# A second level of Strassen's algorithm for four of the seven products of the first GEMM, with the other three in lasting PSUM banks

## The chip, the cores and the metric

The kernel runs on one core of one Trainium2 chip. The metric is the device time of one execution in microseconds (us). The kernel before takes 662.47 us (median of 3 runs, 661.76 to 662.52). "Faster" or "slower" needs 2%. The experiments ran in several rounds, each beside the kernel before, whose median was 662.5 to 664.65 us in them. So a difference of 2 or 3 us between runs of different rounds is not clear of noise.

## The reference, cut to what matters

```python
state = gamma * state + k[t] (outer) v[t]        # retention: 4 batches, 8 heads, 768 steps, head size 64
y[t]  = scale * q[t] @ state
x = y.transpose(0, 2, 1, 3).reshape(3072, 512)   # 3072 tokens, model size 512
h = x @ w_in                                     # first GEMM, 512 -> 2048
g = where(h > 0, h, exp(min(h, 0)) - 1)          # ELU
out = g @ w_out                                  # second GEMM, 2048 -> 512
```

Everything is fp32. The kernel computes the retention in chunks on TensorE, and the two GEMMs in six blocks of 512 tokens each.

## The kernel before

The first block is computed plainly. From the second block on both GEMMs use Strassen's algorithm, in its form with 7 products in place of 8. From the third block on, the second GEMM has a second level of it: each of its seven products (called groups below) is again made of seven small products. The first GEMM has one level, for each quarter n (0 to 3) of the hidden columns. One quarter is this sequence; `use` runs the ELU on a finished result:

```python
def strassen(product, use, between):
    yield
    pa = bank("a"); product(1, pa, True); m1 = kept(pa)          # ScalarE copies M1 out of PSUM
    yield
    pb = bank("b"); product(2, pb, True); use("C11", plus(pb, m1))   # VectorE adds, ELU begins
    yield
    product(6, pa, False); u2 = kept(pa)                         # accumulates M6 on M1
    yield
    pd = bank("d"); product(7, pd, True)
    yield
    product(5, pa, False); u4 = kept(pa); use("C22", plus(pd, u4))
    yield "gap"
    product(3, pa, False); use("C12", pa)
    yield
    product(4, pd, False); h = plus(pd, u2)
    yield "last"
    use("C21", h)
```

So a quarter releases its four ELUs one after the other, and ELUs of one quarter run beside the products of the next. An ELU is two ScalarE instructions (relu, exp) and a last step on VectorE, which is held back until the next ELU. After C12 of a quarter, VectorE makes T3 and T1, inputs of the second GEMM. In the second GEMM one group is (cut):

```python
product(j, 1, pa, True);  m1 = copy(pa)          # ScalarE, 128x128
product(j, 2, pb, True);  add(res[:, 0, 0], pb, m1)
product(j, 6, pa, False); u2 = copy(pa)          # same bank: waits for the copy of product 1
product(j, 7, pd, True)
product(j, 5, pa, False); add(res[:, 1, 1], pd, copy(pa))
product(j, 3, pa, False); nc.scalar.copy(res[:, 0, 1], pa)
product(j, 4, pd, False); add(res[:, 1, 0], pd, u2)
```

## Time and profile before

| | before |
|---|---|
| time, median | 662.47 us |
| TensorE busy | 637.3 us, 97% of the span |
| VectorE / ScalarE / GpSimd busy | 434.7 / 228.3 / 23.8 us |
| TensorE instructions (matmul) | 6144 |
| a block of tokens | 101.7 to 102.9 us |

In the views PE is TensorE (PEld its weight loads), DVE VectorE, ACT ScalarE, POOL GpSimd and L265 a line of that run's kernel. A line of a timeline has the start and length in us, the engine, the line, the operation, the tiles (written <- read), the shapes, and in brackets the idle time before it and what ended it ("issue" where the profile shows nothing). The seam is the place where the first GEMM of a block ends and its second begins.

What the kernel does not do is wait. The view of TensorE's waits of the kernel before says for whom it waited: us in total, how often, the longest. (The whole view has nine rows.)

```profile
PE sc L265 <- DMA qk<-in_qkv_dram: 8.9, 2, 7.5
PE pa L385 <- DVE xb L342: 2.8, 2, 1.4
...
PE pa L618 <- ACT ms L626: 0.4, 1, 0.4
```

The first two rows are the start of the kernel. At the place that this change touches, the second GEMM's wait for ScalarE's small copies (tile `ms`), there is one wait of 0.4 us in the whole run.

### The profile page before, as it was taken

The page shows a single profiled execution, that of the slowest core. Times are in us where ns is not written, and L with a number is a line of the kernel's source. Part 1 is how long each engine was busy: PE and PEld are TensorE (multiplying, and loading weights), DVE is VectorE, ACT ScalarE, POOL GpSimd, SP SyncE. Part 2 cuts the span into 40 slices and gives each one's busy share as a digit, 9 for nine tenths or more (in the row PEclk, how much of TensorE's full clock was granted, in tenths as well). Part 3 has the DMA queues.
Part 4 walks back from the last instruction along what each step waited for, and adds up shares of the span by engine and source line. Part 5 has one row for each costly group of instructions (what it writes and reads, how often), then busy time and mean ns, then how long its engine had stood idle before and what let it go on. Part 6 is the DMA issues. An engine that isn't in the chain of part 4 may idle for free.

```text
span 658.9 us, 14662 instructions
## 1 busy us (share of the span) xinstructions
PE 637.3 (97%) x6144; PEld 537.5 (82%) x6144; DVE 434.7 (66%) x769; ACT 228.3 (35%) x432; POOL 23.8 (4%) x28
## 2 busy tenths in 40 slices
PE   4799999999999999999999999999999999999997
PEld 4664445458888888889999889999889999888996
DVE  5798688566757644549856457867447958355974
ACT  7477542014431002543112554111455111445211
POOL 1000100001100000200000200000100000000000
PEclk9999999999999999999999999999999999999999
DMA  8658977549114757605767703777801768200693
GB/s 342 235 166 289 343 228 232 143 133 376 72 65 160 255 211 257 254 1 174 223 206 254 251 1 95 228 228 253 301 2 42 242 206 267 96 1 20 222 305 126
DMA packets 63825, 123.64 MB, mean 188 GB/s; under 512 B 5136, under 2 KB 22544, under 8 KB 61712
## 3 DMA queue, kind: packets, MB, share of 16 engines
q1 hardware_dynamic: 63760, 122.70, 55.6%
q8 instruction: 49, 0.80, 0.5%
q14 instruction: 16, 0.13, 0.1%
HBM read 100.66 MB, written 22.02 MB: 186 GB/s over the span
## 4 chain that ended last, share of the span: by engine, by line
PE 95%; DVE 2%; DMA 1%; issue 1%; SPq 0%; ACT 0%; DVEq 0%
PE pa L497 21%; PE pa L618 15%; PE pd L497 10%; PE pd L618 8%; PE hp L396 6%; PE pb L497 5%; PE pa L410 4%; PE pa L555 4%; PE pb L618 4%; PE pd L555 2%; PE kv L287 2%; PE pb L410 2%; PE pd L410 2%; PE y L335 2%; PE sc L265 2%; PE y L311 2%
## 5 line engine op out<-in xcount | busy, mean ns | idle before, releaser
L452 DVE TENSOR_TENSOR h<-pd,m 128x512 f32<-128x512 f32 x42 | 29.1, 692 | 86.1 <-ACT m L447 68.6
L447 ACT COPY m<-pa 128x512 f32<-128x512 f32 x63 | 36.3, 577 | 109.7 <-PE pa L497 73.7
L626 ACT COPY ms<-pa 128x128 f32<-128x128 f32 x84 | 22.3, 265 | 125.3 <-PE pa L618 122.3
L374 ACT ACTIVATE r<-r 128x512 f32<-128x512 f32 x96 | 60.5, 630 | 3.0
L618 PE MATMUL pd<-ts,wq 128*128 128x128 f32 x448 | 59.9, 277 | 0.3 <-DVE res L630 0.3
L618 PE MATMUL pa<-ts,wq 128*128 128x128 f32 x448 | 59.2, 275 | 0.0
L373 ACT ACTIVATE r<-h 128x512 f32<-128x512 f32 x60 | 37.9, 631 | 57.2 <-DVE h L452 57.2
L618 PEld LDWEIGHTS pd<-ts,wq 128*128 128x128 f32 x448 | 54.5, 192 | 1.2 <-DVE res L630 0.9
L618 PEld LDWEIGHTS pa<-ts,wq 128*128 128x128 f32 x448 | 54.8, 192 | 0.2
L618 PE MATMUL pa<-gC,wq 128*128 128x128 f32 x384 | 52.0, 278 | 0.4 <-ACT ms L626 0.4
L376 DVE SCALAR_TENSOR_TENSOR gC<-r,h 128x512 f32<-128x512 f32 x60 | 42.1, 701 | 11.3 <-ACT r L374 11.3
L618 PEld LDWEIGHTS pa<-gC,wq 128*128 128x128 f32 x384 | 47.2, 192 | 1.7 <-ACT ms L626 0.5
L239 POOL TENSOR_TENSOR kvn<-kvn,vf 128x512 f32<-128x512 f32 x20 | 21.8, 1089 | 455.7 <-DMA kvn<-in_qkv_dram 455.7
L497 PE MATMUL pa<-xb,w_s 128*128 128x256 f32 x160 | 37.8, 379 | 0.0
L497 PE MATMUL pa<-xb,w_a 128*128 128x256 f32 x160 | 37.8, 379 | 0.0
L497 PE MATMUL pa<-xt,w_s 128*128 128x256 f32 x160 | 37.8, 379 | 0.0
L497 PE MATMUL pb<-xb,w_a 128*128 128x256 f32 x160 | 37.8, 379 | 0.0
L497 PE MATMUL pd<-xt,w_s 128*128 128x256 f32 x160 | 37.8, 379 | 0.0
L497 PE MATMUL pa<-xt,w_b 128*128 128x256 f32 x160 | 37.8, 379 | 0.0
L497 PE MATMUL pd<-xt,w_b 128*128 128x256 f32 x160 | 37.8, 379 | 0.0
L630 DVE TENSOR_TENSOR res<-pd,ms 128x128 f32<-128x128 f32 x56 | 16.1, 287 | 28.8 <-PE pd L618 26.3
L497 PEld LDWEIGHTS pb<-xb,w_a 128*128 128x128 f32 x160 | 30.4, 190 | 4.1
(121 smaller groups left out, 1092.7 us busy)
## 6 DMA issues: line engine op xcount, KB each, us to landing
wq<-scratch_dram SPq DMA_DIRECT2D x196, 256.0 KB, 4.0
wraw<-in_w_dram SPq DMA_DIRECT2D x16, 1024.0 KB, 6.0
qk<-in_qkv_dram SPq DMA_DIRECT2D x24, 512.0 KB, 8.7
kvn<-in_qkv_dram SPq DMA_DIRECT2D x24, 512.0 KB, 9.4
scratch_dram<-so SPq DMA_DIRECT2D x22, 512.0 KB, 3.4
ws<-scratch_dram SPq DMA_DIRECT2D x7, 1024.0 KB, 7.0
scratch_dram<-w_s SPq DMA_DIRECT2D x8, 512.0 KB, 7.3
out_dram<-res SPq DMA_DIRECT2D x12, 256.0 KB, 3.4
```

Of the source, the lines that this page charges most:

```text
L239: eng.tensor_tensor(out=kv[:, 1], in0=kv[:, 1], in1=vf[:, i].unsqueeze(2).to_broadcast([C, H, D]), op=ALU.mult)
L373: nc.scalar.activation(r, h, AF.Relu, scale=-1.0)
L374: nc.scalar.activation(r, r, AF.Exp, scale=-1.0)
L376: later.append(lambda: nc.vector.scalar_tensor_tensor(g, r, -1.0, h, ALU.add, ALU.max))
L396: nc.tensor.matmul(hp, lhsT=w[n][:, fi, j // 2, j % 2, :], rhs=xb[:, j, :], start=(j == 0), stop=(j == 3))
L410: nc.tensor.matmul(ops[d], lhsT=wo[:, row, d * P : (d + 1) * P], rhs=g_plain[row * NF + f], start=(f == 0 and row == 0), stop=(f == NF - 1 ...
L447: nc.scalar.copy(m, ps)
L452: nc.vector.tensor_tensor(out=h, in0=ps, in1=m, op=ALU.add)
L497: nc.tensor.matmul(ps[:, fi, :], lhsT=w[:, fi, j2, :], rhs=x[:, j2, :], start=(begin and fi == 0 and j2 == 0), stop=(j2 == 1), skip_group_ ...
L555: nc.tensor.matmul(ps[:, d, :], lhsT=ws[:, 2 * d + f // 4, f % 4, :], rhs=gq[INPUT2[j]][:, f, :], start=(begin and f == 0 and d == 0), sto ...
L618: nc.tensor.matmul(ps, lhsT=w[:, f, :], rhs=ts[j][k][:, f, :], start=(begin and f == 0), stop=(f == 3), skip_group_check=True,)
L626: nc.scalar.copy(m, ps)
```

## The change

The intent: in the four blocks that have the second level in the second GEMM, give it to M2, M3, M4 and M7 of the first GEMM as well, to save TensorE time. A second-level product covers all four quarters at once, so results no longer come quarter by quarter. M1, M6 and M5 stay in one level and accumulate in four PSUM banks (`qa`), one for each quarter, that last for the whole first GEMM. VectorE adds each bank to the stored partial result when its turn comes (`first_end`), and then the ELU starts. The last VectorE steps of two ELUs are now held back, where it was one (the 2 in `elu(g, g, 2, ...)`). The core of the diff:

```diff
+    TWICE = [2, 3, 7, 4]
+    PLAN = {2: (None, "C11"), 3: (None, "C12"), 7: (None, "C22"), 4: ("C22", "C21")}
+    def first_twice(tb, j):                       # seven small products, as in the second GEMM
+        ...
+    def first_end(n, name, ps):
+        g = gq[name][:, 2 * n : 2 * n + 2, :]
+        nc.vector.tensor_tensor(out=g, in0=ps, in1=g, op=ALU.add)
+        ...
+        return lambda: elu(g, g, 2, combine if name == "C12" else None)
 ...
-        for n in range(NQ):
-            cur = first(n)
 ...
+        for n in range(NQ):
+            qa.append(ps_r.tile([P, 2, TH], FP32, name="qa", tag="r"))
+            first_rest(n, 1, qa[n])               # M1
+        for at, j in enumerate(TWICE):            # M2, M3, M7, M4 in two levels
+            cur = first_twice(tb, j)
+            ...                                   # C11 ends here: its addition and ELU
+        first_rest(0, 6, qa[0])                   # M6, then C21 ends
+        first_rest(1, 6, qa[1])
+        first_end(0, "C21", qa[0])()
+        first_end(1, "C21", qa[1])()
+        sec = second_twice(...); next(sec)        # four subtractions for the second GEMM
+        for n in (2, 3):
+            first_rest(n, 6, qa[n]); first_end(n, "C21", qa[n])()
+        for n in range(NQ):
+            first_rest(n, 5, qa[n])               # M5, then C22 and C12 end
+            for name in ("C22", "C12"):
+                held_elu.append(first_end(n, name, qa[n]))
+                if n < 3:
+                    held_elu.pop()()
+        next(sec)                                 # products 1, 2 of the second GEMM
+        for e in held_elu: e()                    # the last two ELUs
+        next(sec)                                 # products 6, 7
```

(Some lines of it are joined here.) In the second block GpSimd makes the second-level weights and a DMA writes them to DRAM.

## The prediction

> **What bounds the kernel now.** I read the page first (engine shares, chain of waits), then the windows of one block, then the timeline of each engine across the seam between the two GEMMs.
>
> ```profile
> PE 637.3 (97%) x6144; PEld 537.5 (82%) x6144; DVE 434.7 (66%) x769; ACT 228.3 (35%) x432; POOL 23.8 (4%) x28
> ...
> PE 95%; DVE 2%; DMA 1%; issue 1%; SPq 0%; ACT 0%; DVEq 0%
> ```
>
> The second line is the chain that ended last: 95% of the span is TensorE work, so matmul time saved is time saved, as long as nothing else takes its place. The windows below are block 3 (the first of four that change): its first GEMM with a little of the second, then the rest of the second with the retention of the next block. Columns: length, busy us of PE, PEld, DVE, ACT, POOL, clock, DMA share, GB/s.
>
> ```profile
> 251.60:301.70 50.10, 50.10 (x241) 44.34 (x240) 27.13 (x41) 24.85 (x43) 4.17 (x4) 1.00 0.44 158
> 301.70:352.00 50.30, 48.97 (x846) 47.65 (x846) 39.67 (x81) 8.19 (x28) 0.00 (x0) 1.00 0.70 221
> ```
>
> VectorE has 23 us of slack in the first window and 10 us in the second. A block takes 101.7 to 102.9 us (from the starts of consecutive blocks at 251.76, 353.42, 456.07 and 558.95 in the chain). What a product costs is in the starts of consecutive groups on TensorE:
>
> ```profile
> 253.32 1.89 PE L497 MATMUL pb<-xb,w_a 128*128 128x256 f32 x8
> 255.05 1.89 PE L497 MATMUL pa<-xt,w_s 128*128 128x256 f32 x8
> ...
> 304.57 1.06 PE L618 MATMUL pa<-gC,wq 128*128 128x128 f32 x8
> 305.46 1.06 PE L618 MATMUL pb<-gC,wq 128*128 128x128 f32 x8
> ```
>
> Start to start, a product of the one-level form (four fp32 matmuls of 256 columns, eight records) is 1.727 us; one of the two-level form (four of 128 columns) 0.893 us, 3.4% dearer per column.
>
> VectorE and ScalarE pacing, at a later seam:
>
> ```profile
> 400.75 0.69 DVE L452 TENSOR_TENSOR h<-pd,m 128x512 f32<-128x512 f32 x1 [3.06 <-ACT m L447]
> 401.36 0.68 DVE L376 SCALAR_TENSOR_TENSOR gC<-r,h 128x512 f32<-128x512 f32 x1
> 401.96 0.68 DVE L607 TENSOR_TENSOR ts<-gC 128x512 f32<-128x512 f32 x1
> 402.68 0.69 DVE L607 TENSOR_TENSOR ts<-gC,ts 128x512 f32<-128x512 f32 x1
> ...
> 401.48 0.63 ACT L373 ACTIVATE r<-h 128x512 f32<-128x512 f32 x1 [0.76 <-DVE h L452]
> 402.14 0.63 ACT L374 ACTIVATE r<-r 128x512 f32<-128x512 f32 x1
> 402.68 0.25 ACT L626 COPY ms<-pa 128x128 f32<-128x128 f32 x1
> ```
>
> A 512-wide VectorE operation costs 0.61 us start to start, 0.72 if it reads the result of the one before it. A relu starts 0.72 us after the add that feeds it, its exp 0.66 later, the next ScalarE instruction 0.54 after that.
>
> [...] no instruction of either engine stands ahead of program order. So a small copy behind ten ELUs waits for all ten. [...] In this trace 32 score matmuls took 1.13 us right after the 7.50 us wait at the start, 64 of them 1.16 us later on[...]; no idle time later in this trace is longer than 1.5 us. [...] GpSimd worked from 268.23 for 1.04 us, and the subtraction for T3 that started at 268.66 took 1.16 us in place of some 0.7.
>
> **The change part by part.**
>
> *TensorE, removed and added.* Per block the first GEMM had 28 one-level products, 28 x 1.727 = 48.35 us. Now M1, M5 and M6 stay (12 x 1.727 = 20.72) and M2, M3, M4, M7 become 4 x 7 = 28 two-level products of 0.893 (25.00). Together 45.72: 2.63 us less a block, 10.5 us in four blocks. This is all there is to win, bar some small gaps: 1.6%.
>
> *VectorE, added.* Before, per block: 12 sums from PSUM, 16 last steps of ELU, 8 subtractions for T3 and T1, 4 for the inputs: 40 x 0.61 = 24.4 us. After: 12 sums plus 4 lifts with an addend (M4), 16 additions of the lasting banks, 16 ELU ends, 8 and 4 as before, 8 for the inputs of the second level (4 of them in the second GEMM of the block before): 68 x 0.61 = 41.5 us. So about 17 us more, in a first GEMM that is 2.6 us shorter; with the 39.4 of the second GEMM VectorE goes from 64% to about 83% of a block. On average that still fits. Where it lies decides.
>
> *The seam.* Only C11 can be finished early. All twelve ELUs of C21, C22 and C12 come after the last two-level product. Set 0 at its end (M4's product 3). TensorE still has two M6 and four M5 products, 6 x 1.727 = 10.36 us, then products 1 and 2 of the second GEMM, to 12.15. Its product 6 accumulates in the bank of product 1, so it needs ScalarE's copy of product 1. In program order VectorE does from 0.2 on: 1 lift, 4 additions of C21, 4 subtractions for the second GEMM's input, 5 ELU ends (the last of C11, all of C21); 4 additions of C22 and C12 for n = 0 and 1; the ELU ends of C22 and C12 and T3, T1 for n = 0, the ELU end of C22 for n = 1; the addition of C22 for n = 2. That is 24; the 25th is the addition of C12 for n = 2. It starts at 0.2 + 24 x 0.61 + 0.4 (four dependent neighbours) = 15.2. Its relu 15.9, exp 16.6, then the copy at 17.1 to 17.4. TensorE was ready at 12.15: **5.2 us of idle**, each block. Next, the two ELUs that were held back stand before the copy of product 6: five VectorE operations later, at 18.5, comes the addition of C12 for n = 3; relu 19.8 (behind the ELU of C22), exp 20.5, copy 21.0 to 21.3; products 6 and 7 end at 19.2: **2.1 us**. From there VectorE is about 9 us behind and works without pause (inputs, T3 and T1, the four additions into C11, inputs again, the mask of the scores). What TensorE waits for then: C11 before the third group, about 0.3; M2's sums before products 4 and 7 there, 0.45 and 1.05; the next group 0.6: **2.4 us**. With the 8.3 us of a group against some 6 us of VectorE work it has caught up in the fourth or fifth group.
>
> *The middle.* From the first C11 on, ScalarE has relu and exp before the copy of M7's product 1, which must be done before its product 6: addition 0.8 us after the end of M3's product 5, relu +0.72, exp +0.66, copy +0.54, done +0.63 = 3.35, while products 1, 4 and 2 cover 2.68: **0.7 us**. The one-slot distances elsewhere (0.58 us copies in a 0.89 us slot) just hold.
>
> *Sum of one block*: 5.2 + 2.1 + 2.4 + 0.7 = 10.4 lost, 2.6 won: 7.8 longer. Last block: no retention, and it already loses some 3 us to VectorE (the chain of before there goes through the additions into C11 and the inputs twice), so I take 1.5 off: 6.3.
>
> *Second block* (once): weights of the second level are made by GpSimd, 16 operations of 1.09 us or so (its scaling row), in turns with VectorE (up to 0.5 us each on it, where it has 15 us of slack), then 4 MB are written out and the fetch of the first w_out piece waits behind them. The last can be ready near 180, and with 7.0 us to landing comes at about 188 to 191, when it is wanted at 190.6: 0 to 2 us, I take 1. The reads, 16 x 256 KB more a block, are 4.2 MB: 42 GB/s more on 188, with slots at 342 seen; hidden.
>
> Total: 662.5 + 3 x 7.8 + 6.3 + 1 = 693. I go a little under, to 690, because the four small waits after the seam are the least sure.
>
> **The rivals.** *TensorE stays the bound.* If VectorE's extra work hides, the time is 662.5 - 10.5 = 652. For it: 23 us of slack in the first GEMM's window. Against it: the slack is spread evenly there, the new work is not; it would need the m1 copy to pass ten ELUs. *Only the two waits at the seam hurt and VectorE's lag is absorbed*: 4 x (7.3 + 0.7 - 2.6) = +21.6, so 684. *The long idle also drops the clock*: products 6 and 7 at half rate are 1.8 us more, but most of that lies inside the next wait; up to 2 us a block: 700. *Small weights come late*: eleven slots cover 9.8 us against 4.0 us from issue to landing: no wait expected.
>
> **Range and chances.** The two waits at the seam follow from counting instructions; I trust them to 1.5 us a block, hence 6 in all; the lag after it could be half or double (-5, +8). 80%: 672 to 702. A miss would most likely be to the faster side, if an order I read wrongly spares the seam. Over 2% faster needs 649.2, below even the first rival: 0.03. Slower by over 2% is above 675.7: 0.78. Within: 0.19.
>
> **What would show it.** TensorE's share falls from 97% to about 91%. Per block: one idle gap of some 5 us on TensorE released by ScalarE's copy to the small tile, then one of 2 us, behind ELU instructions; in the windows of the second GEMM VectorE busy throughout its first 20 us. Product spacings still 1.727 and 0.893, so that outside the gaps a block has 2.6 us less of TensorE work. VectorE's total about 500 us. I am wrong if those gaps are absent (then about 652), or if the copy is released by TensorE and not by an ELU; if the gaps are there but the groups after them run without waits, it is the second rival.

## The result, and the profile after

The kernel after takes **701.9 us** (median of 4 runs, 701.14 to 702.46), beside 662.5 us (661.76 to 663.42) of the kernel before in the same rounds. The ratio is 1.059 (95% interval 1.0575 to 1.0612): slower. A ratio here is always the mean time of one kernel's runs over that of the other's of the same rounds, so it is not quite the ratio of the medians that are quoted.

Engine shares and the chain of waits of the kernel after, from its page:

```profile
PE 643.2 (92%) x6528; PEld 550.8 (79%) x6528; DVE 510.2 (73%) x881; ACT 229.4 (33%) x432; POOL 47.4 (7%) x44
...
PE 73%; DVE 20%; issue 3%; ACT 2%; DMA 1%; SPq 0%; DVEq 0%
```

VectorE has 75 us more work, and a fifth of the path to the end now leads over it. TensorE's busy time should have fallen by 10 us and rose by 6 (at the half clock, shown below, a product is busy for 2.08 us in place of 1.06). Its waits, same view as above:

```profile
PE pa L765 <- ACT ms L773: 25.0, 9, 5.8
...
PE pa L684 <- ACT m L697: 2.1, 4, 0.5
PE pa L684 <- DVE m L695: 1.8, 3, 0.8
```

The row that stood at 0.4 us now stands at 25.0, and its longest wait is 5.8 us. The span grew from 658.9 to 700.0 us. From the starts of the blocks, the four changed blocks are 9.5, 10.0, 9.8 and 9.4 us longer than before (38.7 together). Block 2 is 0.9 us longer, and the opening of the kernel, which has not changed, 1.5 us.

One changed block, cut into three windows at the two ends of the seam between the GEMMs (columns: length, then busy us of PE, PEld, DVE, ACT, POOL, the clock, DMA share, GB/s):

```profile
365.31:412.30 46.99, 45.23 (x322) 42.40 (x322) 27.61 (x44) 15.24 (x27) 4.42 (x4) 1.00 0.68 223
412.30:429.10 16.80, 10.71 (x56) 9.84 (x55) 15.25 (x26) 11.90 (x22) 0.00 (x0) 0.80 0.22 59
429.10:477.94 48.84, 47.51 (x818) 46.19 (x818) 39.67 (x82) 6.76 (x25) 0.00 (x0) 1.00 0.73 226
```

In the 16.8 us of the seam TensorE works for 10.7 and the clock is 0.80. VectorE is busy for 15.3 of them with 26 instructions. The DMA share is 0.22, so it is no transfer. TensorE across that seam:

```profile
416.31 1.06 PE L765 MATMUL pb<-gC,wq 128*128 128x128 f32 x8
423.19 2.08 PE L765 MATMUL pa<-ts,wq 128*128 128x128 f32 x8 [5.82 <-ACT ms L773]
425.06 1.92 PE L765 MATMUL pd<-ts,wq 128*128 128x128 f32 x8
427.23 2.08 PE L765 MATMUL pa<-ts,wq 128*128 128x128 f32 x8 [0.26 <-ACT ms L773]
429.10 1.15 PE L765 MATMUL pa<-gC,wq 128*128 128x128 f32 x8
```

These are products 2, 6, 7 and 5 of the first group, and product 1 of the next. Product 6 waits 5.82 us for ScalarE's copy. Then products 6, 7 and 5 take 1.87 us each to the start of the next one (425.06 less 423.19, and so on; 7 to 5 has a wait of 0.26 besides), where products of this form are 0.893 us apart at full clock. That is the half clock: the granted clock was 0.50 from 423.2 to 429.1. It costs 3 us more. Now VectorE, GpSimd and ScalarE in the same stretch:

```profile
409.07 1.53 DVE L645 TENSOR_TENSOR ts<-gC 128x512 f32<-128x512 f32 x1
...
420.97 0.68 DVE L740 TENSOR_TENSOR gC<-qa,gC 128x512 f32<-128x512 f32 x1
```

```profile
408.77 1.29 POOL L243 TENSOR_TENSOR kvn<-kvn,vf 128x512 f32<-128x512 f32 x1 [7.37 <-DMA kvn<-in_qkv_dram]
```

```profile
422.35 0.63 ACT L380 ACTIVATE r<-r 128x512 f32<-128x512 f32 x1
422.89 0.25 ACT L773 COPY ms<-pa 128x128 f32<-128x128 f32 x1
```

The operation at 420.97 is the 26th in VectorE's queue after M4, the addition of C12 for n = 2. Its relu and exp follow on ScalarE, and the small copy that TensorE waits for comes right behind. One of the 25 operations before it, a subtraction, took 1.53 us in place of some 0.69: it began while GpSimd was scaling a tile.

### The profile page after: what moved, and what is told of

Its sections match the earlier page's. It is cut to its first block, busy times and chain, and to the rows that moved or that the text cites. A ratio compares the mean times of both kernels' runs of the same rounds, so it can differ in the third digit from the quotient of the medians.

```text
span 700.0 us, 15781 instructions
## 1 busy us (share of the span) xinstructions
PE 643.2 (92%) x6528; PEld 550.8 (79%) x6528; DVE 510.2 (73%) x881; ACT 229.4 (33%) x432; POOL 47.4 (7%) x44
## 4 chain that ended last, share of the span: by engine, by line
PE 73%; DVE 20%; issue 3%; ACT 2%; DMA 1%; SPq 0%; DVEq 0%
PE pa L765 11%; PE pa L684 8%; PE qa L732 7%; PE hp L409 6%; PE pd L765 6%; DVE gC L740 5%; DVE gC L383 4%; PE pa L423 4%; PE pa L568 4%; PE pd L684 3%; DVE ts L645 3%; PE pa L510 3%; PE pb L765 2%; PE pd L568 2%; PE y L339 2%
## 5 line engine op out<-in xcount | busy, mean ns | idle before, releaser
L765 PE MATMUL pa<-ts,wq 128*128 128x128 f32 x448 | 64.7, 291 | 24.6 <-ACT ms L773 24.6
L765 PEld LDWEIGHTS pa<-ts,wq 128*128 128x128 f32 x448 | 58.7, 204 | 26.4 <-ACT ms L773 26.4
L379 ACT ACTIVATE r<-gC 128x512 f32<-128x512 f32 x64 | 40.3, 630 | 59.9 <-DVE gC L740 59.5
L383 DVE SCALAR_TENSOR_TENSOR gC<-r,gC 128x512 f32<-128x512 f32 x64 | 44.9, 711 | 0.0
L740 DVE TENSOR_TENSOR gC<-qa,gC 128x512 f32<-128x512 f32 x64 | 43.2, 681 | 0.1
L684 PE MATMUL pa<-ts,wq 128*128 128x128 f32 x256 | 35.0, 280 | 3.9 <-ACT m L697 2.1
L684 PEld LDWEIGHTS pa<-ts,wq 128*128 128x128 f32 x256 | 31.1, 191 | 5.4 <-ACT m L697 2.8
L645 DVE TENSOR_TENSOR ts<-gC,ts 128x512 f32<-128x512 f32 x48 | 34.5, 720 | 0.8
L645 DVE TENSOR_TENSOR ts<-gC 128x512 f32<-128x512 f32 x48 | 33.6, 701 | 0.0
L423 PE MATMUL pa<-gC,w_s 128*128 128x512 f32 x64 | 30.6, 600 | 0.0
L732 PE MATMUL qa<-xt,w_b 128*128 128x256 f32 x128 | 29.1, 381 | 1.2 <-DVE gC L740 1.2
L732 PE MATMUL qa<-xt,w_s 128*128 128x256 f32 x128 | 29.6, 379 | 0.0
```

What stands on the lines that cost most here:

```text
L379: nc.scalar.activation(e, h, AF.Relu, scale=-1.0)
L383: nc.vector.scalar_tensor_tensor(g, e, -1.0, h, ALU.add, ALU.max)
L423: nc.tensor.matmul(ops[d], lhsT=wo[:, row, d * P : (d + 1) * P], rhs=g_plain[row * NF + f], start=(f == 0 and row == 0), stop=(f == NF - 1 ...
L645: sub = lambda o, x, y: nc.vector.tensor_tensor(out=o, in0=x, in1=y, op=ALU.subtract)
L684: nc.tensor.matmul(ps[:, f, :], lhsT=lhs[f], rhs=xs[j][k], start=(begin and f == 0), stop=True, skip_group_check=True,)
L732: nc.tensor.matmul(ps[:, fi, :], lhsT=w[:, fi, j2, :], rhs=x[:, j2, :], start=(j == 1 and fi == 0 and j2 == 0), stop=(j2 == 1), skip_group ...
```

## The experiments

Each experiment has the kernel after as its base unless it says otherwise. I call the ground plan of the argument "theory A": VectorE and ScalarE take their instructions in program order (in the seam just shown VectorE's 26 operations come in that order, and on ScalarE ten ELUs, from 406.06 to 422.35, stand before the small copy at 422.89), and the small copies stand behind ELUs that stand behind a full VectorE queue. The rivals are the half clock, GpSimd's lock (my word for what the trace shows: a subtraction of 1.53 us beside a GpSimd operation of 1.29 us, in place of some 0.69), the matmul saving itself being illusory, and the bare amount of VectorE's work.

### e1_warm: is it the half clock?

```diff
+                idle = bank("d")[:, 0, 0:P]
+                for f in range(22):               # dummy matmuls, result overwritten
+                    nc.tensor.matmul(idle, lhsT=w_a[0][:, 0, 0, 0, :], rhs=xb[:, 0, 0:P], start=True, stop=True, ...)
```

The dummies fill the gap before product 6.

> The changed kernel with 22 idle matmuls of 128 columns (4.9 us by the spacing of 0.223 us) between products 2 and 6 of the second GEMM's first group, into a bank that product 7 overwrites, so that TensorE has no long gap there. My theory: the half clock after the gap (three products at 1.87 us instead of 0.89 in the changed kernel) is a consequence that mostly lies inside a second wait: product 5 still has to wait for ScalarE's copy of product 6, which stands behind the two ELUs held back, so the products after the gap run at 0.89 but about 2.2 us of idle come back before product 5. Gain about 1 us a block, 4 in all: 698. Rival: the lost clock is a cost of its own, 2.9 us a block: 690.

Measured: correct, 703.96 us (703.25 to 704.96), ratio 1.0611 (1.0575 to 1.0647). TensorE at the seam:

```profile
423.81 1.16 PE L765 MATMUL pa<-ts,wq 128*128 128x128 f32 x8 [0.91 <-ACT ms L773]
427.85 1.16 PE L765 MATMUL pa<-ts,wq 128*128 128x128 f32 x8 [2.00 <-ACT ms L773]
```

Products 6 and 7 are now busy for 1.16 and 1.06 us, in place of 2.08 and 1.92, and TensorE is at product 5 so early that the second wait appears with 2.00 us. From product 1 of the first group to product 1 of the second it is 12.81 us, against 13.68 in the kernel after, so the half clock cost 0.87 us a block there and not 3. The rest of its 3 us lay inside a wait that would have come anyway. The whole did not get faster at all (703.96 beside 701.9 us). The gain of some 3.5 us was eaten elsewhere, by waits that the profile names "issue" (1.30, 1.00 and 0.68 us in one block); what ate the rest was not shown. So theory A was right at the seam and wrong in the sum; the half clock is a symptom, and a small one.

### e2_early: move TensorE's products, leave the queues

```diff
+        next(sec)                    # products 1, 2 of the second GEMM ahead of M5
         for n in range(NQ):
             first_rest(n, 5, qa[n])
+            if n == 1:
+                next(sec)            # products 6, 7 in the middle of M5
             ...
-        next(sec)
-        for e in held_elu: e()
-        next(sec)
```

> The changed kernel with the first group of the second GEMM issued earlier: its products 1 and 2 before the four M5 products, 6 and 7 in the middle of them, so that the copies of products 1 and 6 stand before most ELUs in ScalarE's queue. Same work, other order. My theory: what bounds the seam is the amount of VectorE work in one piece, so the wait only moves: none before product 6, but 3 to 5 us before the second group's product 6, whose inputs VectorE makes after the same row of operations; only the half clock and some idle time of VectorE are won: about 695 (690 to 699). Rival: the copy stuck behind ten ELUs in ScalarE's queue is the cause, and with it all of 5.8 idle, 0.3 and 2.9 of half clock go, 9 us a block: 666.

Measured: correct, 698.81 us (697.49 to 701.00), ratio 1.0536 (1.0494 to 1.0578). That is inside the range, near its slow end. The wait was not removed, it moved to the group's product 3, which stands behind products 1 and 2 of the next group:

```profile
425.74 2.07 PE L765 MATMUL pa<-gC,wq 128*128 128x128 f32 x8 [4.75 <-ACT ms L773]
```

That product needs the copy of product 5, which now stands behind the held ELUs. Giving TensorE other work first does not help while the copies sit at the end of the same queue.

### e3_narrow and e4_twice: less and more VectorE work at the seam

The first of them makes the additions of the lasting banks 128 columns wide in place of 512. Its output is wrong, which doesn't matter for the time. The second does the subtraction for T3 twice.

```diff
# e3_narrow
-        nc.vector.tensor_tensor(out=g, in0=ps, in1=g, op=ALU.add)
+        nc.vector.tensor_tensor(out=g[:, 0, 0:P], in0=ps[:, 0, 0:P], in1=g[:, 0, 0:P], op=ALU.add)
# e4_twice
             sub(mine("T3"), mine("C22"), mine("C12"))
+            sub(mine("T3"), mine("C22"), mine("C12"))
```

> Wrong result on purpose: the 16 additions of the lasting banks in each block work on 128 of 512 columns (about 0.20 us by the 128-wide rows instead of 0.61), everything else, order and number of instructions included, as in the changed kernel. My theory (VectorE's time in one piece): ten of the additions lie ahead of the copy, so the gap of 5.8 us shrinks to about 1.7, the clock stays up, the waits after it all but vanish; some 7.6 us a block: 671 (667 to 678). Rival (the number of ELUs ahead of the copy in ScalarE's queue, whatever VectorE costs): no more than 1 or 2 us a block, 695 or more.

> The changed kernel with each of the four T3 subtractions of a block done twice (same result), four more VectorE operations of 0.61 us or a little more. Two of them lie ahead of the copy of product 1, two after it. My theory: from the last two-level product to the third group of the second GEMM VectorE is what TensorE waits for, so each costs its full time: +2.4 to 2.9 us a block, 712. Rival (only the copy of product 1 matters, the rest is absorbed): +1.2 a block, 707. If VectorE's load were hidden: 702.

Measured: e3_narrow 684.07 us (680.33 to 685.21), ratio 1.030. e4_twice 712.21 us (708.50 to 713.26), correct, ratio 1.074. Product 6 of e3 and of e4:

```profile
413.64 2.08 PE L765 MATMUL pa<-ts,wq 128*128 128x128 f32 x8 [3.79 <-ACT ms L773]
```

```profile
422.70 2.07 PE L766 MATMUL pa<-ts,wq 128*128 128x128 f32 x8 [6.55 <-ACT ms L774]
```

Product 6 comes after 3.79 us in the first and 6.55 us in the second. One operation more in the queue ahead of the copy makes the gap 0.73 us longer (5.82 to 6.55), the cost of one dependent operation. This is what theory A asks for, and the time hit the expected 712. (The expectation had counted two operations ahead of the copy; by the trace it is one, the subtraction for n = 0, and the other three come after it.) In e3 the gap fell by only 2.0 us, and 684 is well above the expected 671. With the additions made cheap, the next limit was ScalarE itself: eight of its ELUs then stood back to back, 1.2 us each, from 403.7 to 413.4. So by this trace even a free VectorE would not have closed the gap in this order, because all twelve ELUs of C21, C22 and C12 come at once.

### e6_pool: GpSimd's scaling out of the seam

```diff
-                load((tb + 1) * CPB + at)
-                if at > 0:
-                    scale_v((tb + 1) * CPB + at - 1)
-        if more:
-            scale_v((tb + 1) * CPB + 3)
+                if at < 2:
+                    load((tb + 1) * CPB + 2 * at)
+                    load((tb + 1) * CPB + 2 * at + 1)
+                if at in (1, 2):
+                    scale_v((tb + 1) * CPB + 2 * at - 2)
+                    scale_v((tb + 1) * CPB + 2 * at - 1)
```

> The changed kernel with the next block's loads and GpSimd scalings issued earlier in the first GEMM, so that no GpSimd operation falls among the seam's VectorE operations (in the changed kernel the last one does, and one subtraction for the inputs takes 1.53 us instead of 0.69). My theory: 0.8 us less in the 5.8 us gap of the three blocks that have scalings: about 699.5. Rival (GpSimd's lock costs nothing at the seam): 702.

Measured: correct, 697.24 us (696.26 to 699.91), ratio 1.0482 (1.0443 to 1.0521), 4.7 us under the kernel after and a little better than expected. The subtraction of 1.53 us is back at 0.68, and the wait of 0.45 us before M5 is gone. So is one of 0.80 us before M4's product 6: in the kernel after, a last step of an ELU started at 393.22, beside a GpSimd operation that had started at 393.18, and took 1.56 us in place of 0.68. The gap itself is still 5.69 us in that block, because TensorE comes earlier too. So VectorE operations beside a GpSimd one cost time here; moving the GpSimd ones, with the earlier loads, is worth 4.7 us, about a tenth of the loss.

### e7_once: the new order without the second level

M2, M3, M7 and M4 are computed in one level again, quarter by quarter, but in the order and with the four lasting banks of the kernel after.

```diff
-            cur = first_twice(tb, j)
+            cur = first_once(tb, j)      # four one-level products, a ScalarE copy (M4: a VectorE addition) each
...                                       # the second level's inputs are not made, its weights not fetched
```

> One part of the change alone (right result): M1, M5, M6 in the four lasting banks and the late additions and ELUs as in the changed kernel, but M2, M3, M4 and M7 at one level, 4 products of 1.727 us each in place of 7 of 0.893. TensorE does again 48.35 us of first GEMM a block (+2.6 over the changed kernel); VectorE loses 12 sums and 8 subtractions a block, all of them before the seam. My theory: the order at the seam is what costs, so the gap of some 5 us, the half clock and the waits after it stay; the two small waits in the middle (1.3 us a block) go: 701.9 + 4 x (2.6 - 1.3) = 707 (700 to 710). Rival (the second level's own sums overload VectorE): the waits go with them, 665 to 675.

Measured: correct, 695.35 us (694.50 to 695.80), ratio 1.0457 (1.0425 to 1.0490). It has the same 6144 matmuls as the kernel before and is 31 us slower. Its seam:

```profile
420.47 1.78 PE L787 MATMUL pa<-ts,wq 128*128 128x128 f32 x8 [3.84 <-ACT ms L795]
```

(GpSimd still makes the weights in this run.) The gap is there, with slow products behind it (the next one starts 1.57 us later in place of 0.893). So four fifths of the loss (31.4 of 39.4 us) come from the lasting banks and the order built on them, and not from the second level. Both readings for this run were off. My own 707 had counted on the lost matmul saving as though it had been a gain in this order. But in the kernel after TensorE only reaches the same queue sooner, so the saved time was waited away: the gap is 3.84 us here and 5.82 there.

### e5_spread: another order

The order of the four is M2, M7, M4, M3. The ELUs of C21 and C22 run while M3 is still being computed, quarters 2 and 3 go first, the copies stand ahead of the last ELUs, and the loads and scalings come earlier. Core of the edit:

```diff
-    TWICE = [2, 3, 7, 4]
+    TWICE = [2, 7, 4, 3]
...
+        cur = first_twice(tb, 3)
+        next(cur);  end(0, "C21");  first_rest(2, 5, qa[2]);  end(2, "C22")
+        next(cur);  end(1, "C21");  first_rest(3, 5, qa[3]);  end(3, "C22")
+        next(cur);  next(cur)
+        first_rest(0, 5, qa[0]);  end(2, "C12");  end(0, "C22");  end(3, "C12")
+        first_rest(1, 5, qa[1]);  e22 = first_end(1, "C22", qa[1])
+        next(cur, None)
+        next(sec)                    # products 1, 2 of the second GEMM and the copy of 1
+        e22()
+        next(sec)                    # products 6, 7 and the copy of 6
+        end(0, "C12");  end(1, "C12")
```

> The changed kernel's work in another order (right result): the two-level products run as M2, M7, M4, M3, so that C21's ELUs begin after M4 and C22's run during M3; the parts of C11, C21 and C12 that are complete first (n = 2, 3) are finished first; M5's products are interleaved with M3's; C12 alone, and of it only n = 0, 1, waits for the last product; the copies of products 1 and 6 of the second GEMM stand ahead of the last ELUs; the next block's loads and scalings come earlier. Same number of instructions on VectorE, ScalarE and TensorE. My theory (too much VectorE and ScalarE work in one piece at the seam, not its amount in a block): the gaps of 5.8 us and the half clock go, 1 to 3 us a block are left: 658 (653 to 668). Rival (VectorE's amount, 82 us of a block of 98, is itself too much): 685 or more.

Measured: correct, 674.75 us (674.09 to 675.55), ratio 1.0149 (1.0118 to 1.0181), clock 0.997. That is 27 us under the kernel after, and 17 above the expected 658. What is left in one block:

```profile
412.73 1.16 PE L766 MATMUL pa<-gC,wq 128*128 128x128 f32 x8 [1.10 <-ACT ms L774]
...
420.70 1.31 PE L766 MATMUL pa<-gC,wq 128*128 128x128 f32 x8 [0.64 <-DVE gC L547]
...
425.24 1.16 PE L766 MATMUL pd<-ts,wq 128*128 128x128 f32 x8 [1.13 <-DVE res L778]
...
428.03 1.16 PE L766 MATMUL pd<-ts,wq 128*128 128x128 f32 x8 [0.74 <-DVE res L778]
```

The large gap and the half clock are gone (the mean granted clock is 0.997, in the kernel after 0.980). A block takes 105.06 us, and its waits, the four shown and one of 0.31, are 3.9 us. The order was the main cause, but not all of it. (Of the 27 us some 5 can be due to the earlier loads and scalings, which e6 tried alone.)

### e9_once_spread: the spread order without the second level

This is e5 with M2, M7, M4 and M3 in one level, by the edits of e7.

> e5_spread's order (M2, M7, M4, M3, ELUs spread, loads early) but with M2, M3, M4, M7 in one level again: the four banks and the spread order without the second level. Beside e5 it tells what the second level itself is worth once the order no longer makes the large gap. Theory A (own): the blocks lose the 2.63 us each of saved TensorE time, and win back the part of e5's 3.9 us of waits that comes from the input subtractions and the sums (my estimate 1.5 to 2.5 a block): within 6 us of e5_spread's 674.75, so 669 to 681, best guess 676. Rival B (the second level itself is the loss and the lasting banks are free when spread): 661 to 666, at the kernel before. Rival C (the second level pays in full when spread): 684 or above.

Measured: correct, 686.80 us (686.46 to 688.44), ratio 1.0351 (1.0303 to 1.0400): rival C, against my own guess of 676. Three blocks of e9 take 324.85 us and three of e5 take 316.86 us, from the starts of their first M2 product. The difference is 2.66 us a block, and 2.63 was counted from the spacings of the products. TensorE's listed waits in these three blocks are about the same, 14.0 us in e9 and 13.5 us in e5. So the saving that the change was made for is real and comes through in full or nearly so, once the order lets it. The one-level form has the same waits (4.25 us in the block below), and VectorE's 11 us less a block (463.5 against 507.1 us in the run) do not shorten them. One of them:

```profile
414.46 1.06 PE L788 MATMUL pd<-ts,wq 128*128 128x128 f32 x8
416.11 1.16 PE L788 MATMUL pa<-ts,wq 128*128 128x128 f32 x8 [0.59 <-ACT ms L796]
417.11 1.06 PE L788 MATMUL pa<-gC,wq 128*128 128x128 f32 x8
```

From 414.46 to 417.11 it is 2.65 us for two products, where 2 x 0.893 = 1.79 would do. So a wait listed with 0.59 us costs 0.86 us, 0.27 us more than the idle time that is listed. The wait of 0.52 us in the kernel after costs 0.26 us more (386.49 to 389.06, 2.57 us for two products), the one of 1.10 us in e5 0.27 us more (410.57 to 413.73). I take some 0.27 us for each short wait, as an estimate from these. A block of e9 has seven such places (six waits, and a slow pair of products after one of them).

### e8_spread2: the waits left in e5, one by one

```diff
+                yield "p5"               # product 5 and its copy before the last ELU
+            if j == 2:                   # products 6, 7, 5 before the next group's subtractions
+                next(cur)
+                next(cur)
...
+            while masks:                 # the masks of the retention scores held back until here
+                masks.pop(0)()
```

> e5_spread with the waits left in its blocks attacked one by one: the fifth product of the second GEMM's first group and its copy are issued before the last held ELU; for the group after it, products 6, 7 and 5 are issued before the next group's inputs; the masks of the retention scores (VectorE, 0.6 to 1.3 us each) are held back until after the next group's sums. Same arithmetic as the kernel after. Theory A (order on the in-order engines is what costs): the waits of 1.10, 0.64, 1.13 and 0.74 us in e5's block fall to about 1 us in all, a block goes from 105.1 to about 102.3, and the whole to 664 us (659 to 668), some 38 under the kernel after and level with the kernel before (ratio 0.995 to 1.008). Theory B (VectorE's added amount, 75% busy, keeps TensorE waiting wherever the work is put): the waits move to the next consumer and it stays at 672 us or above.

Measured: correct, 671.21 us (668.82 to 671.89), ratio 1.0104 (1.0070 to 1.0138), 31 us under the kernel after, but not at the kernel before, and between the ranges of the two theories. The waits did fall, to 1.06 us (0.43 and 0.63) in the block below, as theory A said. But the block takes 106.91 us, and its neighbours take 103.15 and 103.40. In the timeline of TensorE:

```profile
419.26 1.31 PE L774 MATMUL pa<-gC,wq 128*128 128x128 f32 x8 [0.63 <-DVE gC L555]
...
432.01 0.48 PE L299 MATMUL kv<-kvn 64*64 64x64 f32 x4 [3.50 <-issue]
432.42 2.07 PE L774 MATMUL pa<-gT,wq 128*128 128x128 f32 x8
```

A wait of 3.50 us "for nothing that the profile shows", and the slow products after it (1.87 us to the start of the next one), cost this block some 5 us. A look at the DMA queues of this run from 429.5 to 430.0 us finds in the middle of that wait:

```profile
q8 instruction: 1, 0.02, 11.5%
```

This is one of the 52 fetches of instructions in the run (0.85 MB, so 16 KB each). TensorE went on 2.5 us after the start of that half microsecond. It is not alone: the 13 kept traces have 51 waits of TensorE of over 0.4 us put down to "issue" (the longest in the kernel before is 1.15 us), and before the end of every one a fetch of 16 KB began, in 43 of them 2.2 to 2.5 us before it, in the other eight 2.6 to 3.3 us before it. On average there is one fetch in 13 us (670 us over 52), and most fetches cause no such wait. All these waits begin in a stage of the retention or within 3 us after one; in such a stage 112 or 128 small matmuls go by in 2.1 to 2.3 us, each with its own weight load (112 loads in 1.94 us at 424.00 in the kernel before). My reading is that the supply of instructions is the cause. No run here was made to show it.

VectorE also has hardly any room left. In 38 us around the seam it is busy for 36.7 us in e8 and for 29.7 us in the kernel before (both windows begin 24.5 us before the first score matmul of the retention; same columns as above):

```profile
392.00:430.00 38.00, 35.30 (x471) 33.07 (x469) 36.70 (x66) 17.08 (x36) 0.00 (x0) 1.00 0.55 165
```

```profile
389.80:427.80 38.00, 37.05 (x472) 34.87 (x471) 29.72 (x55) 13.13 (x30) 0.00 (x0) 1.00 0.43 138
```

That the amount of its work costs time here is not shown by this: in e9 VectorE had less to do and the waits were the same.

### e10_order6 and e11_m3_once: is it still the order, or the amount?

The base is e8. The first puts the second group's last two products ahead of the third group's first one. The second, on top of that, computes M3 in one level.

```diff
# e10_order6
             cur = inner(j)
+            if j == 6:
+                for _ in before:
+                    pass
             next(cur)
# e11_m3_once, besides
-        cur = first_twice(tb, 3)
+        cur = first_once(tb, 3)
```

> e8_spread2 with one edit: the last two products of the second GEMM's second group are issued before the first product of its third group, which waits for the sums of T3 and C11 (0.63 us in three blocks, 2.66 us and two and a half products at about half clock in the last block). Theory: the fill takes about 0.9 us of TensorE's time out of each of those waits and keeps the clock: 0.9 us in each of three blocks, about 3 us in the last, 5.5 us in all, so 665.5 us (661 to 669), level with the kernel before. Rival: VectorE, which ran without a pause for 30 us around this seam in e8's profile, only ends its queue as late as before, and the wait moves to the fourth product's successor: 669 to 672.

> e10_order6 with M3 in one level again, the other three of the changed products in two. It gives TensorE 0.66 us more per block and takes 3 VectorE additions and half of one set of four subtractions (some 3.3 us of VectorE's time per block by e8's rows) away, all of the additions inside the stretch in which VectorE never pauses. If the amount of VectorE's work around the seam is what is left, the time falls to 660 to 664 us; if only the order counts, it is 2 to 3 us above e10.

Measured: e10 673.26 us (670.24 to 675.37), ratio 1.0155 (1.0133 to 1.0176). e11 675.44 us (674.22 to 681.40), ratio 1.0198 (1.0172 to 1.0224). Both are correct. In e10 the wait moved to the second group's product 4, here in one of the ordinary blocks and in the last one:

```profile
420.87 1.16 PE L774 MATMUL pd<-ts,wq 128*128 128x128 f32 x8 [1.55 <-DVE res L786]
...
631.43 2.07 PE L774 MATMUL pd<-ts,wq 128*128 128x128 f32 x8 [3.15 <-DVE res L786]
```

In kind that is the rival (its range was 669 to 672): the small addition of the second group that product 4 waits for stands in VectorE's queue behind the same four additions into C11 as before. (The profiled run of e10 also had an "issue" wait of 3.18 us.) In e11 these two waits are unchanged to the hundredth, 1.55 and 3.15 us, although VectorE had 11.9 us less work in the run (496.5 against 508.4 us). And its profiled run had 8.4 us of "issue" waits in the changed blocks, the longest this one:

```profile
328.92 0.79 PE L299 MATMUL kv<-kvn 64*64 64x64 f32 x35 [3.57 <-issue]
```

So taking VectorE work away where it is not in the queue of that wait did not shorten the wait. The median is 2.2 us above e10's, where the expectation had 2 to 3 us if only the order counts, but the two runs overlap (674.22 to 681.40 and 670.24 to 675.37): that M3's second level is worth 0.66 us a block is not shown by it.

No version beat the kernel before. The best of the changed ones, e8, is 1.0% slower than it, and some 4.6% faster than the kernel after (1.0104 over 1.0593).

## Why the prediction was right or wrong

The prediction said slower, 690 us (672 to 702), and the time is 701.9: the direction is right, the time at the very end of the range. Its sum was 693 and was shaded the wrong way. That the sum came so near is in part luck: the waits at and after the seam were put too high together, and the half clock, the waits in the middle and the lock were left out or put too low. Step by step:

- **TensorE saves 2.63 us a block: right.** The spacings 1.727 and 0.893 us are unchanged, and e5 against e9 showed 2.66 us a block. In the kernel after, none of it reached the end.
- **The first wait at the seam, 5.2 us: right in mechanism.** It is 5.8 us in each of the four blocks (5.83, 5.82, 5.82, 5.69), and it ends with the operation that the prediction named. That is the 26th in VectorE's queue and not the 25th: two last steps of C11's ELUs are held back, and the prediction counted one. It came 16.6 us after M4 (404.34 to 420.97) in place of 15.2; 0.6 us of this is the operation missed, and 0.84 us the subtraction beside GpSimd. The prediction had read that lock in the trace of before (a subtraction of 1.16 us in place of some 0.7), but put no cost on it. That the gap is still only 0.6 us over 5.2 is because TensorE, held up before M5, came later too. e4 confirmed the queue with one operation more ahead of the copy. e3 showed a limit that the prediction did not have: ScalarE's own pace of 1.2 us for each ELU comes right behind VectorE's.
- **The second wait, 2.1 us: mis-sized, the half clock took its place.** It is 0.26 us in the block shown, because the products before it ran at half clock (0.50). In e1, where they are 1.16 and 1.06 us long, it is 2.00 us. The prediction held the drop of the clock for a rival worth up to 2 us a block. The trace of before has one place that speaks for it: 32 score matmuls took 1.13 us right after the 7.50 us wait at the start, about as long as 64 took later (1.16 us), though the view of the granted clock has 1.00 at both. That a wait of some 5 us would slow the products was its estimate. It happened, in all four blocks (product 6 is busy for 2.08 us in each; the clock in windows of 3.9 to 5.9 us from there is 0.55, 0.50, 0.70 and 0.50), and in the block compared with e1 it cost 0.87 us beyond the wait that it covers.
- **Later waits, 2.4 us: too high.** They are 0.59 and 0.73 in the block shown, and 1.46 in the block before it. The prediction counted the right consumers but a lag that was too long, since the slow products gave VectorE time to catch up.
- **The middle, 0.7 us: too low.** It is 0.52 there, and besides 0.80 before M4's product 6, which waits for a lift on VectorE, and 0.45 before M5, where the bank is still being read for C21. These last two were not in the sum. Both go back to a VectorE operation beside a GpSimd one (1.56 us in place of 0.68, and 1.53 in place of some 0.69): without a GpSimd operation there, in e6 and in the last block, neither wait is left. Each of the three also costs, by the estimate above, some 0.27 us more than is listed.
- **The last block, 6.3 us: it was 9.4.** The allowance for "it already loses some 3 us" had no ground: the last block has the same first gap, 5.69 us, and 0.96 and 1.13 us after it.
- **The second block, 1 us: right in size (0.9), wrong in cause.** It was not a late fetch. VectorE ran beside GpSimd's 16 operations for the weights, single operations of 0.7 us took up to 1.7 us there, and TensorE waited 0.57 us for a result of VectorE.
- **Not in the prediction:** the first 16 matmuls of the plain first GEMM took 5.36 us in place of 3.72. In the profiles of all twelve changed kernels they took 5.1 to 6.5 us, after the same 1.4 us wait as in the kernel before. The clock says how: the first of them ran at a granted clock of 0.50 (19.76 to 22.90 in the kernel after), where the kernel before had 1.00. Why the clock was down there stays open.

For the block shown the account closes: the seven listed waits are 9.2 us, some 0.27 us more for each is 1.9, and the half clock 2.9; less the 2.63 saved and the 0.94 us of "issue" wait that this block had before, that is 10.4 us (my estimate), for the 10.0 by which the block is longer.

The rival "TensorE stays the bound" (652) fell with the traces. What the prediction did not ask is which part of the change costs. The runs say it: the lasting banks with their order cost 31 us (e7), the second level in that order 7 to 8 more. With the ELUs spread, the banks cost 22 us (e9), the second level wins 12, and mending single waits another 4 (e8).

What stays open is why the lasting banks still cost 22 us when spread. The waits of e9's block, 4.25 us listed and by my estimate some 6.1 with 0.27 us more for each of seven places, agree with the 5.2 us by which its block (107.89 us) is longer than that of before (102.66 us), which itself has 0.94 us of "issue" wait. But I found no order without these waits: what I moved came back at the next product that reads a result of VectorE.

## What to carry to other kernels

A saving on the bounding engine can be worth nothing when the new order makes the other engines' work come in a lump: ask not how much slack the helper engine has in a stage, but at which instruction its queue is empty again, and which small copy stands at its end. Test the reordering on its own, without the arithmetic saving (e7, e9), before you judge the saving. And when one wait in a queue is mended, look for the next consumer of the same queue, for the wait tends to move there (e2, e10).

## What else the runs measured

- After the 5.82 us wait of the kernel after, products were 1.87 us apart in place of 0.893, at a granted clock of 0.50. What a shorter wait did was not always the same. After waits of 2.66 us products were 1.67 and 1.71 us apart in one run (e8, last block), and after the same wait in e5 1.21 and 1.15 us; after 3.15 us e10's very next product was slow (1.87 us to the next start), in e11 only the one after it (1.00 us, then 1.43 and 1.70). After the wait of 1.4 us at the start of the plain first GEMM the clock was 0.50 in the kernel after and 1.00 in the kernel before.
- A short wait in a stream of fp32 matmuls cost some 0.27 us more than the idle time listed (e9: 0.86 for 0.59). A product of 128 columns is here 3.4% dearer per column than one of 256 (0.893 twice against 1.727 us).
- A subtraction of VectorE took 1.53 us beside a GpSimd operation of 1.29 us, in place of some 0.69. Such delays reached the end of the full queue: with the loads and scalings issued earlier the whole was 4.7 us shorter (e6).
- TensorE waited up to 3.57 us for nothing that the profile shows (e11), and a 16 KB fetch of instructions began 2.2 to 3.3 us before the end of all 51 such waits of over 0.4 us. That the fetches are the cause is my reading, which no run was made to show.
- A VectorE operation that reads the result of the one before it started 0.72 us after it, in place of 0.60 (401.96 to 402.68, and 401.36 to 401.96, in the kernel before).
